# Pooled attention keys in four groups of 32 partitions, pooled copies on ScalarE, and a new instruction order

## The chip, the core and the metric

The kernel runs on one core of one Trainium2 chip. The metric is the device time of one execution in microseconds (us): 299.09 us is the median of three runs before the change (298.9 to 301.79). The engines are named as in the profile: PE (TensorE matmul), PEld (its weight loads), DVE (VectorE), ACT (ScalarE), POOL (GpSimd) and SP (SyncE, which here only issues DMAs).

## What is computed

Inputs are q, k, v of 8 batches, 8 heads, 576 positions and 64 channels, and four matrices of a second stage. Cut to what matters:

```python
q_d, k_d, v_d = mean over groups of 4 positions        # 576 -> 144
out_d   = softmax(q_d @ k_d.T / 8) @ v_d               # pooled attention, 144 x 144 per head
out_up  = repeat(out_d, 4)                             # back to 576 positions
out_loc = softmax(band(q @ k.T / 8)) @ v               # only |i - j| < 4
x = out_up + out_loc                                   # heads side by side: 8 x 576 x 512
theta = x @ w_theta
y = w_tok_r @ (x * cos(theta)) + w_tok_i @ (x * sin(theta))
u = x + y
out = u + relu(u @ w_ch)
```

## The kernel before

All 8 batches run through a software pipeline. Iteration b of the outer loop (b = 0 to 8) works on three batches at once: the attention of batch b, the transposes of q and k of batch b+1 (`turns`), and the second stage's mixing and output of batch b-1. Each stage is a generator that issues a few instructions and yields; a string of letters, one for each step, says which generator goes next. The strings are written out by hand: FIRST for iteration 0, SECOND for 1, PERIOD for 2 to 6, LAST for 7 and END for 8. `pin` (L640) then ties every instruction to the one before it on its engine, so the order of each engine's queue is exactly the order of issue, and every engine takes its queue in that order.

The letters: A (a in iteration 0) is `turns(b+1)`, S `scores`, N `pooled_out`, V `outputs`, T `transposes`, H `phases`, Z `modulate`, X `mix` of batch b-1, R `channels` of b-1, O `store` of b-1, C the casts of loaded inputs of b+2 (POOL), L the loads of b+3 (SP), and W in iteration 0 the loading and transposing of the token matrices.

What the steps of the prediction touch, with lines of the kernel before:

- `turns`, for batches 2 to 7 in 12 steps: four matmuls (L331) transpose 96 positions of q or k and pool them in the same pass into one PSUM bank `pstr`; ACT copies the transposed part (L334), DVE the pooled part (L335) into qdT or kdT. Batches 0 and 1 take eight wider steps (L307, L312). Its last step pools v: five matmuls of 512 columns (L349) in two groups of 90 and 54 pooled positions, each copied by ACT into vd (L355).
- `scores`: pooled scores are 16 matmuls (L368, keys in two groups of 90, the second padded with zeros; queries are 144 columns), taken through Exp by ACT in three instructions (L379 twice, L388). Five band steps follow: eight matmuls (L400), Exp (L408), and two masks on POOL (L421, L423).
- `pooled_out`: two halves of 16 matmuls each, 65 columns wide (L437): 8 heads, 2 key groups. Column 65 gives the softmax's sum. DVE divides (L444, L445).
- `outputs` (psup L462, psloc L467, DVE L474 to L483), `transposes` (xTps L500, DVE L505), `phases` (psth L517, Sin twice on ACT, L524 and L525), `modulate` (DVE L533), `mix` (psu L553, eight steps of ten matmuls, DVE L559), `channels` (psr L573 or L586, psx L578 or L593, Relu on ACT L598), `store` (DVE L608, then DMA).
- PSUM: `w2` gives two tiles of two banks, `w1` four tiles of one bank, each from one pool with that many buffers (L65 to L72).

Of the kernel before, what the change touches and what calls it, by code (L numbers as in the profile page):

```python
# [2 lines left out]

# [5 lines left out]
FP32 = mybir.dt.float32  # L9
BF16 = mybir.dt.bfloat16  # L10
AF = mybir.ActivationFunctionType
ALU = mybir.AluOpType

P = 128
# [21 lines left out]
TP = TR // 4  # L36
TW = TR + TP

KG = [(0, 90), (90, 54)]

OS = [0, 128, 256, 384, 512]
OC = [128, 128, 128, 128, 64]
# [3 lines left out]
def kernel(  # L46
# [15 lines left out]
    work = ctx.enter_context(tc.tile_pool(name="work", bufs=2))  # L62
    xpool = ctx.enter_context(tc.tile_pool(name="xpool", bufs=1))
    moep = ctx.enter_context(tc.tile_pool(name="moep", bufs=2))
    ps2 = ctx.enter_context(tc.tile_pool(name="ps2", bufs=2, space=bass.MemoryType.PSUM))  # L65
    ps1 = ctx.enter_context(tc.tile_pool(name="ps1", bufs=4, space=bass.MemoryType.PSUM))

    def w2(name):
        return ps2.tile([P, 2, 512], FP32, tag="w2", name=name)

    def w1(name, dt=FP32):
        return ps1.tile([P, 512 if dt == FP32 else 1024], dt, tag="w1", name=name)  # L72


    staged = {}
# [39 lines left out]
    for i in range(2):  # L115
        t = const.tile([P, NCH, H, 66], BF16, name=f"v_w{i}")
        nc.vector.memset(t[:, :, :, 64:65], 1.0)
        v_ws.append(t)
    vds = []
    for i in range(2):  # L120

        t = const.tile([90, 2, H, 66], BF16, name=f"vd{i}")
        nc.vector.memset(t[:, 1, :, :], 0.0)
        nc.vector.memset(t[:, 0, :, 64:65], 1.0)
        nc.vector.memset(t[0:54, 1, :, 64:65], 1.0)
        vds.append(t)
    kdTs = []
    for i in range(2):
        t = const.tile([P, 4, 180], BF16, name=f"kdT{i}")
        nc.vector.memset(t[:, :, SD:180], 0.0)  # L130
        kdTs.append(t)

    def cast(b, engines):

# [64 lines left out]


    PU = []
    for lo, hi, sh, w in ((0, 120, 0, 90), (4, 124, 59, 120)):
        r = const.tile([P, w], BF16, name=f"pu{lo}")
        nc.vector.memset(r, 0.25)
        nc.gpsimd.affine_select(out=r, in_=r, compare_op=ALU.is_ge, fill=0.0,
                                base=4 * sh, pattern=[[-4, w]], channel_multiplier=1)
        nc.gpsimd.affine_select(out=r, in_=r, compare_op=ALU.is_ge, fill=0.0,
                                base=3 - 4 * sh, pattern=[[4, w]], channel_multiplier=-1)
        if lo:
            nc.gpsimd.affine_select(out=r, in_=r, compare_op=ALU.is_ge, fill=0.0,  # L210
                                    base=-lo, pattern=[[0, w]], channel_multiplier=1)
        nc.gpsimd.affine_select(out=r, in_=r, compare_op=ALU.is_ge, fill=0.0,
                                base=hi - 1, pattern=[[0, w]], channel_multiplier=-1)
        PU.append(r)

    def pool_mat(g, c):
        o = 0 if c == 0 else 59 - (KS[c] - 360 * g) // 4
        return PU[min(c, 1)][0:KW[c], o:o + KG[g][1]]


    band = []
# [70 lines left out]
    def turns(b):  # L292

        q_tm, k_tm, v_w = inputs[b]
        qT = work.tile([P, 4, S], BF16, tag="qT", name=f"qT{b}")
        kT = work.tile([P, 4, S], BF16, tag="kT", name=f"kT{b}")
        qdT = work.tile([P, 4, SD], BF16, tag="qdT", name=f"qdT{b}")
        kdT = kdTs[b % 2]
        parts[b] = (qT, kT, qdT, kdT)

        pairs = ((q_tm, qT, qdT), (k_tm, kT, kdT))

        def wide_turn(n, hh):
            tm, To, Tdo = pairs[n]
            ps = w2(f"pstr{n}{hh}_{b}")
            for r in range(NTR):
                nc.tensor.matmul(  # L307
                    out=ps[:, r // 3, (r % 3) * TR:(r % 3) * TR + TR],
                    lhsT=tm[:, r, 2 * hh:2 * hh + 2, :], rhs=ip[:, 0:TR], start=True, stop=True,
                )  # L310
            for r in range(NTR):
                nc.tensor.matmul(  # L312
                    out=ps[:, 0, 3 * TR:3 * TR + SD],
                    lhsT=tm[:, r, 2 * hh:2 * hh + 2, :], rhs=pw[:, r, :],
                    start=(r == 0), stop=(r == NTR - 1),
                )
            src = ps[:, :, 0:3 * TR].rearrange("p k (c w) -> p w k c", w=TR)
            dst = To[:, hh, :].rearrange("p (w k c) -> p w k c", k=2, c=3)
            srcd, dstd = ps[:, 0, 3 * TR:3 * TR + SD], Tdo[:, hh, 0:SD]
            if b == 0 and n == 1:  # L320
                nc.vector.tensor_copy(out=dst, in_=src)
                nc.scalar.copy(out=dstd, in_=srcd)
            else:
                nc.scalar.copy(out=dst, in_=src)
                nc.vector.tensor_copy(out=dstd, in_=srcd)

        def turn(n, c):
            tm, To, Tdo = pairs[n]
            ps = w1(f"pstr{n}{c}_{b}")[:, 0:4 * TW].rearrange("p (hh w) -> p hh w", w=TW)
            for hh in range(4):  # L330
                nc.tensor.matmul(  # L331
                    out=ps[:, hh, :], lhsT=tm[:, c, 2 * hh:2 * hh + 2, :], rhs=ip, start=True, stop=True,
                )
            nc.scalar.copy(out=To[:, :, TR * c:TR * c + TR], in_=ps[:, :, 0:TR])  # L334
            nc.vector.tensor_copy(out=Tdo[:, :, TP * c:TP * c + TP], in_=ps[:, :, TR:TW])  # L335

        for i in range(8 if b < WIDE else 12):
            if b < WIDE:
                wide_turn(i % 2, i // 2)
            else:  # L340
                turn(i // 6, i % 6)
            yield

        vd = vds[b % 2]
        for g, cs in ((0, (0, 1, 2)), (1, (3, 4))):
            m = KG[g][1]
            ps = w1(f"psvd{g}_{b}")
            for c in cs:
                nc.tensor.matmul(  # L349
                    out=ps[0:m, :],  # L350
                    lhsT=pool_mat(g, c),
                    rhs=v_w[0:KW[c], c, :, 0:D],
                    start=(c == cs[0]), stop=(c == cs[-1]),
                )
            nc.scalar.copy(out=vd[0:m, g, :, 0:D], in_=ps[0:m, :].rearrange("p (h d) -> p h d", d=D))  # L355
        yield

    pds, pms, xds, xs = {}, {}, {}, {}

    def scores(b):  # L360

        qT, kT, qdT, kdT = parts.pop(b)
        pd = pds[b] = work.tile([90, 2, H, SD], BF16, tag="pd", name=f"pd{b}")
        pms[b] = []

        def pooled_scores(dst, kk, hh):
            for par in range(2):
                nc.tensor.matmul(  # L368
                    out=dst(par),
                    lhsT=kdT[64 * par:64 * par + 64, hh, 90 * kk:90 * kk + 90],  # L370
                    rhs=qdT[64 * par:64 * par + 64, hh, :],
                    start=True, stop=True,
                )

        for kk in range(2):
            ps = w2(f"psSd{kk}_{b}")
            for hh in range(3):
                pooled_scores(lambda par: ps[0:90, par, SD * hh:SD * hh + SD], kk, hh)
            nc.scalar.activation(  # L379
                out=pd[:, kk, 0:6, :].rearrange("p (j e) w -> p e j w", e=2),  # L380
                in_=ps[0:90, :, 0:3 * SD].rearrange("p e (j w) -> p e j w", w=SD),
                func=AF.Exp, scale=SCL,
            )
            yield
        ps = w2(f"psSd2_{b}")
        for kk in range(2):
            pooled_scores(lambda par: ps[0:90, par, SD * kk:SD * kk + SD], kk, 3)
        nc.scalar.activation(  # L388
            out=pd[:, :, 6:8, :].rearrange("p k e w -> p e k w"),
            in_=ps[0:90, :, 0:2 * SD].rearrange("p e (k w) -> p e k w", w=SD),  # L390
            func=AF.Exp, scale=SCL,
        )
        yield
# [34 lines left out]
    def pooled_out(b):  # L428
# [3 lines left out]
        for g in range(2):  # L432
            ps = w2(f"psnd{g}_{b}")
            pv = ps[:, :, 0:260].rearrange("p e (j w) -> p e j w", w=65)
            for h in range(H):
                for kk in range(2):
                    nc.tensor.matmul(  # L437
                        out=pv[0:120, h // 4, h % 4, :],
                        lhsT=pd[:, kk, h, 24 * g:24 * g + 120],
                        rhs=vd[:, kk, h, 0:65],  # L440
                        start=(h % 4 == 0 and kk == 0), stop=(h % 4 == 3 and kk == 1),
                    )
            rd = work.tile([120, 2, 4], FP32, tag="rd", name=f"rd{g}_{b}")
            nc.vector.reciprocal(out=rd, in_=pv[0:120, :, :, 64])  # L444
            nc.vector.tensor_tensor(  # L445
# [157 lines left out]
    def store(b):  # L603
# [14 lines left out]


    FIRST = (  # L620
        "aWallaWaaalaSlllaWlaccSSNcWSWlcNSlcVSVlAlVcSAAcklTTlkkWVSWTAcAHWTVAHWcZHccWTkkZAkCckWkkkZCHWAkWCCWHC"
        "WLLLCAZLLWLWWCCZCLWLLLL"
    )
    SECOND = (
        "ASAXSAXSAXANSXAXAVASXSXSNTROSAACXRCAAOVRHOTVCVHLTVCRLHTZTCLCHZZHCLZRZOLOCCSLLLLL"
    )
    PERIOD = (
        "SSXXAXSAASAANXANASAAXVSAAXSTCVXASCCVHXCCTVROHTCVRLOHTRZHOTCCLLRLZOZZHCRZSOLLLLLL"
    )
    LAST = (  # L630
        "SSXXXSSXNSXSVXSVTXSVRHONTXTVHVSHTRTZOZROHZHZZRORO"
    )
    END = (
        "XXXXXXXROROXRORROO"
    )

    last = {}
# [68 lines left out]
```

## Time and profile before

| what | value |
|---|---|
| median of 3 runs | 299.09 us |
| the profiled execution | 298.93 us |
| its span, first to last instruction | 297.2 us |
| mean granted TensorE clock | 0.976 of full speed |
| busy: PE, DVE, ACT, POOL | 275.5, 204.1, 189.7, 159.5 us |

The page also cuts the span into 40 slices of 7.43 us; a digit is the busy share in tenths, and PEclk is the granted clock in tenths:

```profile
DVE  4433868657895598658883888468855986488642
ACT  1145458775668776776788667877787678565312
POOL 5666774478841399327960798059904900580000
PEclk9998579999999999999999999999999999999999
DMA  7999999999999953897189906992220012000304
```

The clock fell to about half between 30 and 37 us and was full afterwards. The DMA engines are full for the first 16 slices, while inputs of the first batches are fetched ahead. Durations of matmuls in the profile run from start to a modelled end and overlap; what a matmul costs PE is the distance from its start to the start of the next.

### The profile page before, as it was taken

To read this page: it belongs to the slowest core of one execution; us is meant where nothing else is said; L and a number is where in the kernel's file an instruction comes from. 1 tells how busy PE (TensorE), PEld (TensorE's weight loads), DVE (VectorE), ACT (ScalarE), POOL (GpSimd) and SP (SyncE) were. 2 spreads that over 40 slices of the span, in tenths; PEclk is the share of its full clock that TensorE was granted. 3 is DMA by queue.
4 is the path that set the end of the run, shared out by engine and by line. 5 is a ranking of instruction groups with operands and counts; after the bars stand their busy time and mean duration, and the time that the engine had idled before them with its cause. 6 is when DMAs were issued, how large, how long until landed. Compare 5 with 4: busy or idle time off the path is not lost.

```text
span 297.2 us, 7393 instructions
## 1 busy us (share of the span) xinstructions
PE 275.5 (93%) x2946; PEld 197.4 (66%) x2946; DVE 204.1 (69%) x466; ACT 189.7 (64%) x304; POOL 159.5 (54%) x186
## 2 busy tenths in 40 slices
PE   2497899999989999999999999999999999999993
PEld 1385587687656876587657876687668766776762
DVE  4433868657895598658883888468855986488642
ACT  1145458775668776776788667877787678565312
POOL 5666774478841399327960798059904900580000
PEclk9998579999999999999999999999999999999999
DMA  7999999999999953897189906992220012000304
GB/s 188 228 298 276 254 198 189 256 195 200 186 253 188 235 109 102 180 224 144 36 199 218 199 5 181 216 208 46 79 82 3 3 67 94 2 35 3 124 23 138
DMA packets 107826, 43.57 MB, mean 147 GB/s; under 512 B 97424, under 2 KB 101520, under 8 KB 107792
## 3 DMA queue, kind: packets, MB, share of 16 engines
q1 hardware_dynamic: 107792, 43.10, 69.4%
q8 instruction: 23, 0.38, 0.6%
q14 instruction: 11, 0.09, 0.1%
HBM read 33.65 MB, written 9.44 MB: 145 GB/s over the span
## 4 chain that ended last, share of the span: by engine, by line
PE 75%; DMA 7%; POOL 4%; SPq 4%; DVE 4%; ACT 2%; issue 1%; DVEq 0%; POOLq 0%; ACTq 0%
PE psu L553 26%; PE psth L517 11%; PE psr L573 8%; PE pstr L331 6%; PE psnd L437 4%; PE psS L400 3%; DMA q<-in_q_dram 3%; PE psvd L349 3%; SPq L107 3%; PE psloc L467 3%; PE psup L462 3%; PE xTps L500 2%; DMA w<-in_moe_w_theta_dram 2%; PE psx L578 2%; PE psSd L368 2%
## 5 line engine op out<-in xcount | busy, mean ns | idle before, releaser
L553 PE MATMUL psu<-WT,z 120*128 120x288 bf16 (+1 forms) x640 | 87.0, 286 | 0.2 <-ACT rel L598 0.2
L421 POOL TENSOR_SCALAR_AFFINE_SELECT pm<-pm 128x1024 bf16<-128x1024 bf16 (+1 forms) x32 | 33.7, 1053 | 73.7 <-ACT pm L408 73.6
L553 PEld LDWEIGHTS <-z 120*128 120x128 bf16 (+1 forms) x640 | 59.9, 98 | 15.9 <-issue 0.2
L408 ACT ACTIVATE pm<-psS 128x1024 bf16<-128x1024 f32 (+1 forms) x40 | 39.4, 984 | 18.0 <-PE psS L400 16.7
L559 DVE TENSOR_TENSOR uT<-psu,xT 128x288 bf16<-128x288 f32 x64 | 29.0, 454 | 26.2 <-PE psu L553 25.9
L517 PE MATMUL psth<-wth,xT 128*120 128x512 bf16 (+1 forms) x160 | 41.3, 381 | 0.2 <-DVE xT L505 0.2
L524 ACT ACTIVATE cs<-psth,pihc 120x512 bf16<-120x512 f32 (+1 forms) x40 | 27.4, 686 | 16.0 <-PE psth L517 13.8
L598 ACT ACTIVATE rel<-psr 128x512 f32<-128x512 f32 (+1 forms) x40 | 22.0, 554 | 23.1 <-PE psr L573 19.7
L423 POOL TENSOR_SCALAR_AFFINE_SELECT pm<-pm 128x1024 bf16<-128x1024 bf16 (+1 forms) x32 | 34.1, 1064 | 2.2
L573 PE MATMUL psr<-wch,uT 128*128 128x512 bf16 x128 | 33.0, 378 | 0.0
L608 DVE TENSOR_TENSOR osb<-rel,psx 128x512 f32<-128x512 f32 (+1 forms) x40 | 24.9, 630 | 7.6 <-ACT rel L598 7.6
L533 DVE TENSOR_TENSOR z<-cs,x 120x1024 bf16<-120x1024 bf16 (+1 forms) x40 | 29.2, 756 | 0.8 <-ACT cs L525 0.8
L476 DVE TENSOR_TENSOR tmp<-psloc,rl 120x512 bf16<-120x512 f32 (+1 forms) x40 | 27.6, 691 | 1.4
L483 DVE TENSOR_TENSOR x<-tmp,psup 120x512 bf16<-120x512 bf16 (+1 forms) x40 | 27.4, 686 | 1.4
L525 ACT ACTIVATE cs<-psth 120x512 bf16<-120x512 f32 (+1 forms) x40 | 23.5, 588 | 0.0
L517 PEld LDWEIGHTS <-xT 128*120 128x120 bf16 (+1 forms) x160 | 18.0, 131 | 7.9 <-DVE xT L505 0.7
L153 POOL CAST v_w<-v 128x1024 bf16<-128x1024 f32 x16 | 18.4, 1166 | 7.7 <-DMA v<-in_v_dram 5.2
L149 POOL CAST k_tm<-k 96x1024 bf16<-96x1024 f32 x18 | 18.3, 1040 | 7.7 <-DMA k<-in_k_dram 7.7
L334 ACT CAST kT<-pstr 128x384 bf16<-128x384 f32 x36 | 16.0, 483 | 9.8 <-PE pstr L331 9.8
L467 PEld LDWEIGHTS <-pm 128*128 128x128 bf16 (+1 forms) x320 | 16.6, 105 | 7.0 <-DVE tmp L476 1.9
L335 DVE CAST qdT<-pstr 128x96 bf16<-128x96 f32 x36 | 9.2, 256 | 16.1 <-ACT qT L334 14.8
L334 ACT CAST qT<-pstr 128x384 bf16<-128x384 f32 x36 | 16.2, 484 | 4.9 <-PE pstr L331 4.9
(89 smaller groups left out, 474.4 us busy)
## 6 DMA issues: line engine op xcount, KB each, us to landing
v<-in_v_dram SPq DMA_DIRECT2D x32, 256.0 KB, 5.8
out_dram<-osb SPq DMA_DIRECT2D x32, 256.0 KB, 2.2
q<-in_q_dram SPq DMA_DIRECT2D x36, 192.0 KB, 4.8
k<-in_k_dram SPq DMA_DIRECT2D x36, 192.0 KB, 5.1
q<-in_q_dram SPq DMA_DIRECT2D x8, 288.0 KB, 4.8
k<-in_k_dram SPq DMA_DIRECT2D x8, 288.0 KB, 6.9
v<-in_v_dram SPq DMA_DIRECT2D x8, 200.0 KB
wt<-in_moe_w_tok_r_dram SPq DMA_DIRECT2D x4, 288.0 KB, 6.9
```

The source lines that it names most:

```text
L334: nc.scalar.copy(out=To[:, :, TR * c:TR * c + TR], in_=ps[:, :, 0:TR])
L408: nc.scalar.activation(out=pv, in_=ps[0:kw].rearrange("p e (j w) -> p (e j) w", w=P)[:, :, 0:qn], func=AF.Exp, scale=SCL,)
L421: nc.gpsimd.affine_select(out=pv, in_=pv, compare_op=ALU.is_ge, fill=0.0, base=off, pattern=[[0, 8], [-1, qn]], channel_multiplier=1)
L423: nc.gpsimd.affine_select(out=pv, in_=pv, compare_op=ALU.is_ge, fill=0.0, base=6 - off, pattern=[[0, 8], [1, qn]], channel_multiplier=-1)
L476: nc.vector.tensor_tensor(out=tmp[0:cnt].rearrange("p (j e d) -> p e j d", e=2, j=4), in0=pv[0:cnt, :, :, 0:D], in1=rl[0:cnt].unsqueeze(3) ...
L483: nc.vector.tensor_tensor(out=x[0:cnt], in0=tmp[0:cnt], in1=up[0:cnt], op=ALU.add)
L517: nc.tensor.matmul(out=th[0:cnt, :], lhsT=xT[:, dc, QS[c]:QS[c] + cnt], rhs=wth[:, dc, :], start=(dc == 0), stop=(dc == 3),)
L524: nc.scalar.activation(out=cs[0:cnt, 0, :], in_=th[0:cnt], func=AF.Sin, bias=pihc[0:cnt], scale=1.0)
L533: nc.vector.tensor_tensor(out=z[0:cnt, c, :, :], in0=css.pop((b, c))[0:cnt], in1=xs[b][c][0:cnt].unsqueeze(1).to_broadcast([cnt, 2, DM]), ...
L553: nc.tensor.matmul(out=ps[:, 0:288], lhsT=z[0:QC[c], c, ri, P * dc:P * dc + P], rhs=WT[0:QC[c], ri, c, cols], start=(c == 0 and ri == 0), ...
L559: nc.vector.tensor_tensor(out=uT[:, dc, cols], in0=ps[:, 0:288], in1=xT[:, dc, cols], op=ALU.add)
L573: nc.tensor.matmul(out=psr, lhsT=uT[:, dc, P * c:P * c + P], rhs=wch[:, dc, :], start=(dc == 0), stop=(dc == 3),)
```

## The change

Pooled keys are laid out in four groups of 32 partitions. Groups 0 to 3 hold 30 pooled keys each (120 of 144), and the last 24 form a fifth group, whose scores for heads 0 to 3 and 4 to 7 are stacked in four blocks of 32 partitions. The matching values are a block diagonal (`vd[:, 1]`): POOL multiplies the pooled values of the last chunk by `own`, which is 1 on a head's own 32 partitions and 0 elsewhere.

- Pooling v: four matmuls with 32 output partitions and 512 columns (L354), each into its own 32 partitions, and four with 128 columns (L357). ACT copies twice (L359 512 wide, L361 128 wide), POOL multiplies twice (L363).
- Pooled scores: eight matmuls with 128 keys (L382) and eight with 32 keys (L402). Exp is two instructions (L392, L408) in place of three.
- Pooled output: each half has eight matmuls of 65 columns (L456) and two of 260 (L462).
- Pooled copies of `turns` go from DVE to ACT (L338); kdT is now one plain buffer, from which DVE makes the padded kdP in two copies (L347, L348).
- PSUM: two tags of one buffer for `w2` and four for `w1`, taken in a fixed cycle.
- All five order strings are new. In iteration 0 the load of w_ch now comes ahead of v of batch 1 and q of batch 2; before, it came after both. In PERIOD each engine's queue is new too; two places are used below. At the end of a period PE's queue is the last psth, psr, psx, psr, psx, psr (L610), psx, psva (L354), psvb (L357), one pstr, psSd (L382), one pstr, then psu. DVE's is z twice, osb, z twice, osb three times, the two kdP copies, then uT.

```diff
-KG = [(0, 90), (90, 54)]
+KP = 32
...
+    turn2, turn1 = itertools.cycle("ab"), itertools.cycle("abcd")
     def w2(name):
-        return ps2.tile([P, 2, 512], FP32, tag="w2", name=name)
+        return ps2.tile([P, 2, 512], FP32, tag="w2" + next(turn2), name=name)
...
-            nc.vector.tensor_copy(out=Tdo[:, :, TP * c:TP * c + TP], in_=ps[:, :, TR:TW])
+            nc.scalar.copy(out=Tdo[:, :, TP * c:TP * c + TP], in_=ps[:, :, TR:TW])
...
+        nc.vector.tensor_copy(out=kdP[:, :, 0:4, 0:30], in_=kdT[:, :, 0:120].rearrange("p h (g m) -> p h g m", g=4))
+        nc.vector.tensor_copy(out=kdP[:, :, 4, 0:24], in_=kdT[:, :, 120:144])
+        yield
         vd = vds[b % 2]
-        for g, cs in ((0, (0, 1, 2)), (1, (3, 4))):
...
+        psa, psb = w1(f"psva_{b}"), w1(f"psvb_{b}")
+        for c in range(4):
+            nc.tensor.matmul(out=psa[KP * c:KP * c + KP, :], lhsT=PU[min(c, 1)], rhs=v_w[:, c, :, 0:D],
+                             start=True, stop=True)
+        for c in range(4):
+            nc.tensor.matmul(out=psb[KP * c:KP * c + KP, 0:2 * D], lhsT=PU[1][0:KW[4], :],
+                             rhs=v_w[0:KW[4], 4, c::4, 0:D], start=True, stop=True)
+        nc.scalar.copy(out=vd[:, 0, :, 0:D], in_=psa.rearrange("p (h d) -> p h d", d=D))
+        nc.scalar.copy(out=last4, in_=psb[:, 0:2 * D].rearrange("p (s d) -> p s d", d=D))
+        for s in range(2):
+            nc.gpsimd.tensor_tensor(
+                out=vd[:, 1, 4 * s:4 * s + 4, 0:D],
+                in0=last4[:, s, :].unsqueeze(1).to_broadcast([P, 4, D]),
+                in1=own.unsqueeze(2).to_broadcast([P, 4, D]),
+                op=ALU.mult,
+            )
...
-                    lhsT=kdT[64 * par:64 * par + 64, hh, 90 * kk:90 * kk + 90],
+                    lhsT=kdP[64 * par:64 * par + 64, hh, 0:4, :],
...
+        for h in range(H):
+            par, r = h % 2, KP * (h % 4)
+            nc.tensor.matmul(
+                out=ps[r:r + KP, h // 4, SD:2 * SD],
+                lhsT=kdP[64 * par:64 * par + 64, h // 2, 4, :],
+                rhs=qdT[64 * par:64 * par + 64, h // 2, :],
+                start=True, stop=True,
+            )
...
             for h in range(H):
-                for kk in range(2):
...
+                nc.tensor.matmul(
+                    out=pv[0:120, h // 4, h % 4, :],
+                    lhsT=pd[:, h, 24 * g:24 * g + 120], rhs=vd[:, 0, h, 0:65],
+                    start=(h % 4 == 0), stop=False,
+                )
+            for e in range(2):
+                nc.tensor.matmul(
+                    out=pv[0:120, e, :, :],
+                    lhsT=pd[:, H + e, 24 * g:24 * g + 120], rhs=vd[:, 1, 4 * e:4 * e + 4, 0:65],
+                    start=False, stop=True,
+                )
...
     PERIOD = (
-        "SSXXAXSAASAANXANASAAXVSAAXSTCVXASCCVHXCCTVROHTCVRLOHTRZHOTCCLLRLZOZZHCRZSOLLLLLL"
+        "ASAXXSSAXSAANAXVSXAVSCAXASTTVAHNXVHTXASTZHVRCHCOTRZZAOLHCSCLCCLCLLLZZRROCOROLLLL"
     )
     END = (
-        "XXXXXXXROROXRORROO"
+        "XXXXXXXXRORORORORO"
     )
```

## The prediction

> **What bounds the kernel now.** First the page's busy table, then the same by stretches of the span (the bounds taken from the chain of waits, where a new period begins with the matmuls of L349), then PE's own waits.
>
> ```profile
> PE 275.5 (93%) x2946; PEld 197.4 (66%) x2946; DVE 204.1 (69%) x466; ACT 189.7 (64%) x304; POOL 159.5 (54%) x186
> ```
> ```profile
> 80.00:90.00 10.00, 8.72 (x78) 4.91 (x78) 9.74 (x20) 6.98 (x12) 4.35 (x5) 1.00 1.16 237
> ...
> 154.33:185.67 31.34, 31.34 (x351) 22.39 (x352) 23.32 (x55) 23.71 (x40) 19.82 (x19) 1.00 0.77 155
> ```
> ```profile
> PE pstr L307 <- DVE q_tm L143: 4.8, 1, 4.8
> PE pstr L307 <- DVE qdT L325: 3.5, 2, 2.9
> ```
>
> In the stretches the columns are length, then busy time of PE, PEld, DVE, ACT, POOL, granted clock, DMA share, GB/s. In a period (iterations 2 to 6) PE is busy 31.34 of 31.34 us at full clock, ACT 23.71, DVE 23.32. PE's large waits are all in the first 14 us; from about 50 to 290 us only 80 to 95 us shows gaps, about 2 us in all, while DVE is at 9.74 of 10. So a microsecond taken from PE's queue in a period shortens the run, unless another engine then comes late.
>
> What PE's steps cost is read from start to start in PE's timeline of one period (start, duration, engine, line):
>
> ```profile
> 153.59 0.63 PE L586 MATMUL psr<-wch,uT 128*64 128x256 bf16 x8
> 154.05 0.28 PE L593 MATMUL psx<-ident,uT 128*64 128x128 bf16 x4
> 154.26 1.39 PE L349 MATMUL psvd<-v_w,pu 128*90 128x512 bf16 x5
> 155.58 0.57 PE L368 MATMUL psSd<-qdT,kdT 64*90 64x144 bf16 x12
> 156.09 2.63 PE L553 MATMUL psu<-WT,z 120*128 120x288 bf16 x20
> ...
> 160.08 0.32 PE L368 MATMUL psSd<-qdT,kdT 64*90 64x144 bf16 x4
> 160.34 0.59 PE L331 MATMUL pstr<-ip,q_tm 96*128 96x120 bf16 x8
> ...
> 161.63 1.02 PE L437 MATMUL psnd<-vd,pd 90*120 90x65 bf16 x16
> 162.48 1.39 PE L553 MATMUL psu<-WT,z 120*128 120x288 bf16 x10
> 163.71 0.37 PE L331 MATMUL pstr<-ip,q_tm 96*128 96x120 bf16 x4
> 163.92 1.02 PE L437 MATMUL psnd<-vd,pd 90*120 90x65 bf16 x16
> 164.78 0.38 PE L331 MATMUL pstr<-ip,k_tm 96*128 96x120 bf16 x4
> ```
>
> Pooling v costs 155.58 - 154.26 = 1.32 us, pooled scores 0.51 + 0.26 = 0.77, pooled output 0.85 + 0.86 = 1.71: 3.80 us of each period. Two prices come out too. Twenty matmuls of 288 columns before L331 take 158.55 - 156.09 = 2.46 us, 0.123 each or 0.427 ns a column. And L586, eight matmuls of 256 columns into alternating halves of the output partitions, takes 0.46 us where 8 x 256 x 0.427 is 0.87: matmuls into different output partitions do run side by side here.
>
> **The change on PE, per batch.** *Pooling v*: four matmuls of 512 columns, one after another, would be 0.87 us and four of 128 columns 0.22, 1.09 together; at L586's ratio (0.46/0.87) 0.58; side by side four ways 0.27. I take 0.45, nearer to the four-way end because four groups are addressed where L586 has two. It saves 0.87 (0.23 to 1.05). *Pooled scores*: L368 costs 0.51/12 = 0.0425 us a matmul; sixteen at that price are 0.68. The eight narrow ones could be as quick as 0.24 in all (four pairs of 61 ns, 144 columns each) or as slow as 0.49 (one after another). It saves 0.09 (-0.06 to 0.19). *Pooled output*: a 65-column matmul costs 0.855/16 = 0.053; eight of them and two of 260 columns (0.111 each) are 0.65 a half, 1.30 for both. It saves 0.41; the bound is 0.3 to 0.45. Together 1.37 us a batch, between 0.5 and 1.7.
>
> One rule speaks against the narrow scores. The Trainium skill, "TensorEngine Tiling (Array Packing)", section "Restrictions and Gotchas", says that matmuls on different row halves must write different PSUM banks and cannot use one bank at once. In the code L368 sends its two row halves to two banks, while the new L402 sends both to the same bank. If that makes the eight run singly, by the column price above they cost 0.49 and not 0.34, 1.0 us over seven batches, and the sum would be 293.8 in place of 292.8; no trace here shows two row halves in one bank.
>
> Batches 1 to 7 do this work where PE is the bound (L349 of batch 1 starts at 54.9 us), so 7 x 1.37 = 9.6 us (3.3 to 11.8). Batch 0 does it around 20 to 30 us; there the chain of waits goes through DMA and POOL, and I count nothing.
>
> **Other engines.** ACT gains 12 copies of 96 elements a period and DVE loses them:
>
> ```profile
> L334 ACT CAST qT<-pstr 128x384 bf16<-128x384 f32 x36 | 16.2, 484 | 4.9 <-PE pstr L331 4.9
> ...
> L335 DVE CAST qdT<-pstr 128x96 bf16<-128x96 f32 x36 | 9.2, 256 | 16.1 <-ACT qT L334 14.8
> ```
>
> ACT's 576-wide copy (L324) takes 640 ns and the 384-wide one 484, 0.81 ns an element, so 96 elements are about 250 ns; two copies in a row took 0.85 us, not 0.97, so up to 0.1 overlaps. That is 1.9 to 3.0 us. One Exp of 884 ns goes, and the second v copy shrinks from 579 to about 270: 1.2 us off. ACT stands at 24.4 to 25.5 of some 30 us, not the bound. DVE loses 12 x 0.256 = 3.1 us and gains two kdP copies; nearest are 0.40 us (480 elements from PSUM, L505) and 0.15 (96 elements, L186), so 0.2 to 0.55, taken as 0.4. POOL gains two products of 256 elements, between 0.26 (L205, 90 elements) and 0.62 us (L233, 512) each; POOL idles 9.31 us at the start of a period before its first mask, and psnd, which needs them, comes after four psu: hidden. If POOL were late, its masks would be as well. Exchanging the buffers' tags takes nothing: the same eight banks are used in turn.
>
> **The new wait.** At a period's end DVE is now in PE's way. psSd (L382) needs kdP, and kdP stands on DVE behind the last osb. Laying the new queues out with the durations above, from the end of the last psth (t=0): ACT's two Sin take until 1.3; DVE's last z until 2.0; three osb (0.6, 0.6, 0.35) until 3.65; kdP until 4.05. PE: psr, psx, psr, psx, the last psr and psx are 0.86+0.22+0.86+0.22+0.46+0.21 = 2.83, then psva and psvb 0.45 and pstr 0.24: 3.52. PE waits about 0.5 us, and everything in its queue behind (pstr, psu) with it. If z or osb runs ahead by 0.6 it is nothing; if they run behind, or the handovers take 0.1 each, 0.9. Over the six starts of iterations 2 to 7: 3.0 us back (0 to 5.4). If pooling v does not run side by side, PE arrives later by that time and this wait vanishes: the two uncertainties partly cancel.
>
> **The first two iterations.** w_ch, 1.05 MB, now goes ahead of v of batch 1 and q of batch 2. The 2.4 MB of v and q were issued from 36.0 and cast on landing by 54.0, 133 GB/s; w_ch and two pieces of k, 1.44 MB, were there at 59.1, 282 GB/s. So it delays them 3.7 to 7.9 us. Against it: five pieces of q and k of batch 1 now stand ahead of the seventh token-matrix piece, at which the SP queue stood from 21.9 to 25.7 (3.8 us), and q of batch 2 was cast by 55.05 and first wanted at 57.19 (2.1). I take 0.5 us lost, near where delay and cover meet, between 2 gained and 5.8 lost (7.9 less 2.1). Iteration 1 has its eight psu early and then a tail where DVE (psnd, x, xT, osb, z: some 17 us against 15 of PE) paces: its gaps of 2 us stay, no more and no less, within 1 us. END's first psr now follows all eight psu; nothing waits there that did not.
>
> **Sum**, against the profiled execution of 298.93 (1.73 beyond its span; 0.16 below the median): 298.93 - 9.6 + 3.0 + 0.5 = 292.8.
>
> **Rivals.** (1) *No new wait* (0.25): DVE, relieved of its copies, is ahead and kdP is in time: 298.93 - 9.6 + 0.5 = 289.8. For it: DVE has slack in a period; against: the last three osb depend on the last psr. (2) *Narrow matmuls do not run side by side* (0.17): pooling v and scores save 0.2 together, pooled output 0.42: 7 x 0.6 = 4.2, no wait for kdP, 0.5 for the loads: 295.2. Against: L586. (3) *ACT becomes the pace, slower* (0.06): ACT idles 31.34 - 23.71 = 7.6 us a period. If its order forces all of that, a period is 24.4 to 25.5 + 7.6 = 32 to 33.1, 0.7 to 1.8 over the old, and six such periods with 0.5 for the loads give 303 to 310; say 305. It decides once forced idle exceeds 6.9 us. Against: PE ends most of ACT's idle time, and PE's pace itself shortens. (4) The change does not lower PE's work at all, because weight loads or switching between shapes eat it: 298 to 300 (0.05), for it that the columns streamed stay 6,944 a batch, against it L586 and the nine matmuls fewer a batch.
>
> **How the numbers follow.** Forecast 0.47, with 290.5 to 295; the others as given. About 1% (3 us) is what a measurement can tell from no change: faster needs less than 296.1. All of the forecast but a tail, rival 1, and two thirds of rival 2 lie there: 0.82. Same: the rest of rival 2, rival 4, tails: 0.12. Slower 0.06. The range of 288 to 297.5 takes in forecast and rivals 1 and 2, with the bounds of the loads.
>
> **What would show it.** psva to the next pstr at 0.3 to 0.6 us; psnd at 0.65 a half; PE waiting for DVE kdP six times at about 0.5; a period of 30.0 to 30.7; ACT near 25 in it. A period over 31 with ACT above 27 proves me wrong by rival 3; a PE gap of several us near 55 to 60 is the loads.

## The result and the profile after

| | before | after |
|---|---|---|
| median, us (4 runs each) | 299.19 | 309.58 |
| lowest to highest, us | 298.9 to 301.79 | 307.51 to 312.5 |
| ratio to before, 95% interval | | 1.030 [1.023, 1.038] |
| profiled execution, us | 298.93 | 309.22 |
| a middle period, us | 31.34 | 34.20 |

The kernel became 3% slower, where 292.8 us had been forecast. The ratio goes by means and leaves out the execution of 312.5 us, which was in a slower state that some executions show, so it isn't the quotient of the medians. The first view is the page: busy time by engine, and the granted clock in 40 slices, now of 7.69 us.

```profile
PE 273.9 (89%) x2865; PEld 195.7 (64%) x2874; DVE 207.1 (67%) x423; ACT 192.6 (63%) x368; POOL 168.2 (55%) x203
...
PEclk9999999599999999799998999799989999999999
```

PE does a little less than before in a longer span, and the clock now falls five times: deeply in the eighth slice (54 to 61 us), and then once about every 34 us, that is once a period. The stretch of one period, from the start of pooling v (L354) to its next start (columns as in the prediction's table of stretches), and PE's waits (total, times, longest) say the same:

```profile
124.72:158.92 34.20, 32.03 (x343) 22.64 (x341) 24.11 (x45) 24.67 (x50) 20.96 (x23) 0.95 0.72 142
```
```profile
PE psx L617 <- DVE osb L632: 8.4, 4, 2.1
...
PE psSd L382 <- DVE kdP L347: 0.5, 1, 0.5
```

PE has gaps of 34.20 - 32.03 = 2.17 us in a period that had none, and the large wait is not the one that was forecast: psx, not psSd, waits, four times 2.1 us. The timeline around it (start, duration, engine, line; in brackets the idle time just before and what ended it) shows where the time goes, first PE, then DVE and POOL:

```profile
121.75 0.63 PE L610 MATMUL psr<-wch,uT 128*64 128x256 bf16 x8
124.49 0.30 PE L617 MATMUL psx<-ident,uT 128*64 128x128 bf16 x4 [2.11 <-DVE osb L632]
124.72 0.40 PE L354 MATMUL psva<-v_w,pu 128*32 128x512 bf16 x4
125.09 0.24 PE L357 MATMUL psvb<-v_w,pu 100*32 100x128 bf16 x4
125.26 0.38 PE L334 MATMUL pstr<-ip,q_tm 96*128 96x120 bf16 x4
125.62 0.36 PE L382 MATMUL psSd<-qdT,kdP 64*128 64x144 bf16 x6
125.91 0.58 PE L334 MATMUL pstr<-ip,q_tm 96*128 96x120 bf16 x4
126.28 4.08 PE L577 MATMUL psu<-WT,z 120*128 120x288 bf16 x20
130.29 0.24 PE L382 MATMUL psSd<-qdT,kdP 64*128 64x144 bf16 x2
130.46 0.31 PE L402 MATMUL psSd<-qdT,kdP 64*32 64x144 bf16 x8
130.70 0.40 PE L420 MATMUL psS<-qT,kT 64*128 64x128 bf16 x8
...
117.67 1.27 DVE L557 TENSOR_TENSOR z<-cs,x 120x1024 bf16<-120x1024 bf16 x2
...
119.49 4.35 DVE L557 TENSOR_TENSOR z<-cs,x 120x1024 bf16<-120x1024 bf16 x2
123.76 1.60 DVE L632 TENSOR_TENSOR osb<-rel,psx 128x512 f32<-128x512 f32 x3
...
118.85 3.01 POOL L161 CAST k_tm<-k 96x1024 bf16<-96x1024 f32 x3 [6.21 <-PE pstr L334]
121.80 2.94 POOL L165 CAST v_w<-v 128x1024 bf16<-128x1024 f32 x2
```

The new arithmetic is as quick as forecast: pooling v, from 124.72 to 125.26, costs 0.54 us. Ahead of it PE stands for 2.11 us. The narrow psx (L617), the transposed last piece of u, needs a PSUM bank that the first of the three osb (DVE's sums of rel and psx for the output) empties, and these stand on DVE behind two z that take 4.35 us; the two z before them took 1.27. During those 4.35 us POOL casts k and v of the batch two ahead without a pause. POOL had idled 6.21 us until a matmul of L334 released it: it may overwrite k_tm only when PE has transposed the last piece of k out of it. The page's group of z shows the loss as a mean, 1084 ns where it had been 756:

```profile
L557 DVE TENSOR_TENSOR z<-cs,x 120x1024 bf16<-120x1024 bf16 (+1 forms) x40 | 42.3, 1084 | 1.4 <-ACT cs L549 1.3
```

The gap costs a second time. The twenty psu behind it go from 126.28 to 130.29, 4.01 us where they had taken 2.46 (granted clock 0.50 from 126 to 129): 1.6 us more. 34.20 - 2.1 - 1.6 = 30.5 is the period that was forecast.

### The profile page after: what moved, and what is told of

Same layout as the page of the kernel before. It is cut to its first block, busy times and chain, and to the rows that moved or that the text cites. A ratio compares the mean times of both kernels' runs of the same rounds, so it can differ in the third digit from the quotient of the medians.

```text
span 307.5 us, 7263 instructions
## 1 busy us (share of the span) xinstructions
PE 273.9 (89%) x2865; PEld 195.7 (64%) x2874; DVE 207.1 (67%) x423; ACT 192.6 (63%) x368; POOL 168.2 (55%) x203
## 5 line engine op out<-in xcount | busy, mean ns | idle before, releaser
L577 PE MATMUL psu<-WT,z 120*128 120x288 bf16 (+1 forms) x640 | 94.0, 302 | 0.1
L577 PEld LDWEIGHTS <-z 120*128 120x128 bf16 (+1 forms) x640 | 63.9, 103 | 19.5 <-issue 0.3
L557 DVE TENSOR_TENSOR z<-cs,x 120x1024 bf16<-120x1024 bf16 (+1 forms) x40 | 42.3, 1084 | 1.4 <-ACT cs L549 1.3
L622 ACT ACTIVATE rel<-psr 128x512 f32<-128x512 f32 (+1 forms) x40 | 22.2, 554 | 17.7 <-PE psr L597 16.4
L165 POOL CAST v_w<-v 128x1024 bf16<-128x1024 f32 x16 | 20.2, 1276 | 9.8 <-DMA v<-in_v_dram 8.6
L337 ACT CAST kT<-pstr 128x384 bf16<-128x384 f32 x36 | 17.2, 478 | 7.0 <-PE pstr L334 6.9
L337 ACT CAST qT<-pstr 128x384 bf16<-128x384 f32 x36 | 17.8, 495 | 5.5 <-PE pstr L334 5.5
L363 POOL TENSOR_TENSOR vd<-last,own 128x256 bf16<-128x256 bf16 x16 | 9.8, 635 | 20.6 <-ACT last L361 20.6
```

Source lines behind the costliest of these rows:

```text
L557: nc.vector.tensor_tensor(out=z[0:cnt, c, :, :], in0=css.pop((b, c))[0:cnt], in1=xs[b][c][0:cnt].unsqueeze(1).to_broadcast([cnt, 2, DM]), ...
L577: nc.tensor.matmul(out=ps[:, 0:288], lhsT=z[0:QC[c], c, ri, P * dc:P * dc + P], rhs=WT[0:QC[c], ri, c, cols], start=(c == 0 and ri == 0), ...
```

## The experiments

The theory after the first look: the new PERIOD puts the last step on k so late that POOL's casts fall beside DVE's z, z waits for POOL, PE waits for osb, and the clock falls after that wait. The rivals: it is the wait for kdP, it is the clock alone, it is the fixed turn of the PSUM banks, or it is the loads of the first iterations. Ratios are to the kernel before, run on the same chip.

| kernel | median, us | ratio [95%] | middle period, us |
|---|---|---|---|
| a1_old_period | 308.62 | 1.024 [1.014, 1.033] | 32.74 |
| a2_k_buffers | 296.83 | 0.989 [0.981, 0.996] | 30.57 |
| a3_fill | 306.21 | 1.018 [1.011, 1.026] | 32.59 |
| a4_before_new_period | 347.36 | 1.158 [1.149, 1.167] | 41.0 |
| b1_early_turn | 303.01 | 1.008 [1.003, 1.012] | 32.2 |
| b2_before_late_turn | 318.19 | 1.049 [1.038, 1.060] | 36.0 to 37.3 |
| v1_w_ch_later | 295.82 | 0.984 [0.978, 0.989] | 30.57 |
| u1_pooled_copies_dve | 301.96 | 1.005 [1.001, 1.009] | 31.3 |
| u2_psum_pools | 294.57 | 0.981 [0.976, 0.986] | 30.40 |
| v2_vd_on_dve | 296.41 | 0.981 [0.974, 0.988] | 30.56 |
| c1_after_pools | 311.48 | 1.036 [1.032, 1.040] | 34.16 |
| c2_pools_w_ch_k_buffers | 294.73 | 0.979 [0.975, 0.984] | 30.4, one of 32.2 |

**Two buffers for k** (the kernel after, one word changed):

```diff
-        k_tm = work.tile([TR, NTR, H, D], BF16, tag="k_tm", bufs=1, name=f"k_tm{b}")
+        k_tm = work.tile([TR, NTR, H, D], BF16, tag="k_tm", bufs=2, name=f"k_tm{b}")
```

> The kernel after with two buffers for k_tm, so that POOL's casts of k need not wait for the last k turn on PE (24.7 us of waiting in the trace). Theory: the casts of k and v run some 6 us earlier, beside the first z and not the last; z3 and z4 fall to 0.7 us, the wait at psx goes or falls under 1 us, 294 to 302. Rival (z is slow for another reason than POOL): z3 stays at 2.9 us, 308 to 311.

It took 296.83 us, 12.8 less than the kernel after in these medians. Order and arithmetic are those of the kernel after; only what POOL must wait for is different. Its timeline at the same place, POOL, DVE and PE:

```profile
113.67 3.46 POOL L161 CAST k_tm<-k 96x1024 bf16<-96x1024 f32 x3
...
121.18 0.68 DVE L557 TENSOR_TENSOR z<-cs,x 120x1024 bf16<-120x1024 bf16 x1
...
123.36 0.30 PE L617 MATMUL psx<-ident,uT 128*64 128x128 bf16 x4
123.59 0.40 PE L354 MATMUL psva<-v_w,pu 128*32 128x512 bf16 x4
...
125.19 2.62 PE L577 MATMUL psu<-WT,z 120*128 120x288 bf16 x20
```

The casts of k now start at 113.67, 9.92 us ahead of psva; in the kernel after they start 5.87 ahead. The z beside no cast takes 0.68, psx waits for nothing, and the twenty psu take 2.56 at full clock. The period is 30.57 us, in the forecast's 30.0 to 30.7. POOL still collides with z (882 ns on average), but with earlier z, and PE hardly waits for what stands behind those. The release of k_tm is therefore the cause of the loss in the periods.

**The gap filled** (the kernel after, 36 matmuls into an unused half of the same PSUM bank between L610 and psx for batches 1 to 5, which is at the end of iterations 2 to 6, so that PE works where it had waited; at the end of iteration 6 it had not waited):

```diff
+                for i in range(36 if 1 <= b <= 5 else 0):
+                    hf = i % 2
+                    nc.tensor.matmul(
+                        out=psr[64 * hf:64 * hf + 64, w:2 * w], lhsT=uT[:, 0, 512:576],
+                        rhs=wch[:, 0, 0:w], start=True, stop=True,
+                    )
```

> 36 extra matmuls (256 columns, alternating halves, into the unused half of the psr bank, read by nobody) stand between L610 and the last psx in iterations 1 to 5, some 2 us of PE work where PE sat idle 2.1 us. Theory (the idle gap makes the granted clock fall to half for some 3.3 us, which costs 1.6 us at each of four period starts): the clock stays at 1.0 at the period starts, the 20 psu that took 4.08 us take 2.5, the time is 302 to 304. Rival (the clock falls for some other reason, such as the load of the matmuls itself): the 20 psu stay at 4.0, the time is 309 or more.

The total missed its 302 to 304: 306.21. The period answered: 32.59 us (127.71 to 160.30) against 34.20, 1.61 less, at a granted clock of 1.00 throughout. So of the 3.63 us that two buffers gained per period (34.20 - 30.57), 1.61 were the clock and 2.0 the wait itself. Less came of it in all, for three reasons. Iteration 1, which has no filling, took 40.53 us and not 39.18: its psvb waited 2.39 us for POOL's cast of v, where the profile of the kernel after shows a wait of 0.31. Iteration 2 took 34.49 and not 32.94: at its start the clock fell behind waits of 1.26 and 0.36 us. And in iteration 6 the 36 matmuls filled no gap and cost 1.96 us.

**The old order in the new kernel**, and **the new order in the old one** (each takes the PERIOD of the other):

```diff
-        "ASAXXSSAXSAANAXVSXAVSCAXASTTVAHNXVHTXASTZHVRCHCOTRZZAOLHCSCLCCLCLLLZZRROCOROLLLL"
+        "SSXXAXSAASAANXANASAAXVSAAXSTCVXASCCVHXCCTVROHTCVRLOHTRZHOTCCLLRLZOZZHCRZSOLLLLLL"
```

> The kernel after with only the PERIOD string of the kernel before. Theory: the casts end before most of z, no wait at psx; but psSd now stands right behind psva, and kdP on DVE behind three z and the last osb, so PE waits 1.5 to 2 us for kdP at each period start, with or without a fall of the clock: 295 to 303. Rival (the new work itself is slow, whatever the order): 308 to 311 with the same wait at psx.

> The kernel before with only the PERIOD string of the kernel after. Theory (the order is at fault: the last k turn stands late, so POOL's casts of k and v run beside DVE's z, z takes up to 2.9 us, osb and then PE's psx come late): z is slow here too, PE waits about 2 us at psx at the period's end, 304 to 310 us. Rival (the new matmuls, the copies on ACT or the padded keys are at fault, the order is innocent): 298 to 301.

With the old order the collision is gone (z is back at 723 ns on average) and psx waits no longer, but the time was 308.62, a miss. Other waits took the place of the first, as PE's waits show:

```profile
PE psSd L382 <- DVE kdP L347: 5.9, 6, 1.2
...
PE psr L597 <- ACT cs L549: 3.5, 5, 0.7
```

The first is the wait that the prediction had named, here 1.0 us a period: the old order has psSd directly behind psvb, with no pstr between them. The old order was written for a kernel without kdP, and doesn't suit the new one. The clock falls at two of the six starts of periods: in iteration 2 behind waits of 1.56 and 0.67 us, and in iteration 6 behind 0.30 and 1.01 us, while the same two waits in the three iterations between left it at 1.00.

The reverse exchange gives no evidence on the order in its total of 347.36 us: the old `scores` has one step more, so each later S of the string means another instruction, and psloc alone waits 23.7 us for masks. Two details can be used. psx waits for osb there too, four times 2.2 us, with z at 936 ns. And what the clock does is not a matter of a wait's length alone, as PE's waits within one period show:

```profile
165.23 0.55 PE L467 MATMUL psloc<-v_w,pm 100*96 100x65 bf16 x8 [2.87 <-POOL pm L423]
175.03 0.30 PE L593 MATMUL psx<-ident,uT 128*64 128x128 bf16 x4 [2.23 <-DVE osb L608]
...
190.12 0.42 PE L467 MATMUL psloc<-v_w,pm 128*128 128x65 bf16 x8 [1.74 <-POOL pm L423]
```

The granted clock is 1.00 from 160 to 190 us, behind the waits of 2.87 and 2.23 us, and 0.50 from 191 to 193, behind the one of 1.74. It is the same in the other three periods with these waits.

**One letter of each PERIOD.** The last A of the string is the step of `turns` that transposes the last piece of k. In the new kernel it goes directly behind the A before it; in the old kernel it goes to a late place, nothing else.

```diff
-        "...VHTXASTZHVRCHCOTRZZAOLHC..."
+        "...VHTXAASTZHVRCHCOTRZZOLHC..."
```
```diff
-        "...AAXSTCVXASCCVHX...LLRLZOZZHCRZSO..."
+        "...AAXSTCVXSCCVHX...LLRLZOZZAHCRZSO..."
```

> The kernel after with one letter of PERIOD moved: the last k turn goes right behind the one before it, some 5 us earlier in PE's queue; k_tm keeps one buffer. Theory (where this turn stands decides when POOL may cast k, and so beside which z): as with two buffers, the wait at psx goes, the clock stays full at the period starts, a period is 30.5 to 31 us, the time 295 to 300. Rival (a second buffer helped through the loads that it lets go earlier, not through the casts): 306 to 311.

> The kernel before with one letter of PERIOD moved: the last k turn goes 24 letters later, to where the kernel after has it; nothing else. Theory: the casts of k and v land on the last z here too, z and osb run late, PE waits at the end or start of each period and the clock falls behind a wait of 2 us: 306 to 320. Rival (only the new work or the rest of the new order is at fault): 298 to 301.

The early step gave 303.01 us, between the two forecasts: psx waits no longer and the clock doesn't fall at the start of a period, but the casts now lie beside z of the first blocks, x comes late behind them, and xTps waits for DVE's x 8.3 us in seven places. The collision moved, and a part of the loss stayed.

The late step made the old kernel, with its old arithmetic, 5% slower: 318.19 us. Its timeline shows the whole chain in a kernel that has no kdP, no narrow matmuls and no turn of the banks (POOL, DVE, PE):

```profile
154.10 3.01 POOL L149 CAST k_tm<-k 96x1024 bf16<-96x1024 f32 x3 [5.79 <-PE pstr L331]
...
154.95 4.14 DVE L533 TENSOR_TENSOR z<-cs,x 120x1024 bf16<-120x1024 bf16 x2
159.02 0.24 DVE L335 CAST kdT<-pstr 128x96 bf16<-128x96 f32 x1
...
159.32 0.59 PE L349 MATMUL psvd<-v_w,pu 128*54 128x512 bf16 x2 [2.30 <-DVE kdT L335]
...
160.54 4.05 PE L553 MATMUL psu<-WT,z 120*128 120x288 bf16 x20
```

A late last k step releases the casts, two z take 4.14 us, PE waits 2.30 and then runs its twenty psu at half clock (3.89 us to the next start). At 0.6 us each the two z would have been through before PE needed kdT. One letter of the order is enough for it.

**The prices by themselves.** A small program of its own: eight z alone, beside six casts of POOL, beside six masks; eight osb beside six casts; then PE in blocks of 64 matmuls with pauses of known length between them.

> A probe that leaves the whole computation out. First part: eight DVE products shaped like z (bf16, both inputs in SBUF) alone, beside six POOL casts shaped like k's, beside six POOL masks; then eight sums shaped like osb (fp32, one input in PSUM) beside six casts. Theory (z and POOL's casts cannot run at once): alone z takes 0.6 to 0.7 us; beside the casts the two take turns, some z of 1.5 to 3 us, and both together last about the sum of both, 10 us and more; osb beside casts stays at 0.6 to 0.7. Rival (both slow down each other evenly): every z near 1.2 us, osb too. Second part: PE works 13 us, pauses for one to five ACT copies, and works again, twice over. Theory: pauses of 0.8 and 1.4 us leave the clock full, pauses over 2 us halve it for some 3 us; in between it depends on when the pause falls. Rival: no pause under 3 us has any effect.

The timeline of DVE and POOL, then of PE, where 13.97 us is a block at full clock:

```profile
10.13 4.90 DVE L71 TENSOR_TENSOR z<-cs,x 120x1024 bf16<-120x1024 bf16 x8
...
15.51 9.83 DVE L71 TENSOR_TENSOR z<-cs,x 120x1024 bf16<-120x1024 bf16 x8
...
25.83 10.22 DVE L71 TENSOR_TENSOR z<-cs,x 120x1024 bf16<-120x1024 bf16 x8
...
36.54 4.86 DVE L77 TENSOR_TENSOR osb<-rel,psx 128x512 f32<-128x512 f32 x8
...
15.35 8.24 POOL L82 CAST k<-k 96x1024 bf16<-96x1024 f32 x6
...
36.37 5.93 POOL L82 CAST k<-k 96x1024 bf16<-96x1024 f32 x6
...
37.86 13.97 PE L107 MATMUL wk<-ch,lh 128*128 128x512 bf16 x63 [1.32 <-ACT ch L115]
53.80 13.97 PE L107 MATMUL wk<-ch,lh 128*128 128x512 bf16 x62 [1.97 <-ACT ch L115]
70.40 15.66 PE L107 MATMUL wk<-ch,lh 128*128 128x512 bf16 x63 [2.62 <-ACT ch L115]
...
135.28 15.66 PE L107 MATMUL wk<-ch,lh 128*128 128x512 bf16 x63 [1.97 <-ACT ch L115]
153.56 13.97 PE L107 MATMUL wk<-ch,lh 128*128 128x512 bf16 x63 [2.62 <-ACT ch L115]
```

A z costs 0.61 us alone (4.90/8). Beside casts the eight take 9.83, but the casts end at 23.59, and two of the z run after them; the six beside them took (9.83 - 2 x 0.61)/6 = 1.43 each. Six casts take 8.24 us beside z and 5.93 beside osb, which itself isn't touched (0.61). z and casts together last from 15.35 to 25.34, 9.99 us, little less than the two one after the other, 4.90 + 5.93 = 10.83: they nearly take turns, as the theory had it, and both sides lose. A pause of 1.97 us cost nothing the first time and 15.66 - 13.97 = 1.69 us the second; 2.62 cost 1.69 the first time and nothing the second. These 1.69 us are about the 1.6 that the periods of the kernel after pay.

**Loads of the first iterations.** On top of the two buffers for k, w_ch's load goes behind q of batch 2:

```diff
-        nc.sync.dma_start(out=w32[1], in_=moe_w_ch.rearrange("(c p) e -> p c e", p=P))
...
+                if ri == 1 and c == 0:
+                    nc.sync.dma_start(out=w32[1], in_=moe_w_ch.rearrange("(c p) e -> p c e", p=P))
```

> Two buffers for k_tm as in the run a2, and w_ch is loaded behind q of batch 2, as in the kernel before. Theory (w_ch ahead of v of batch 1 and q of batch 2 makes their casts and PE's first steps of iteration 1 late, and the gap halves the clock for some 6 us): no clock fall near 56 us, 3 to 5 us less than a2, 291 to 294. Rival (DMA has room, the fall near 56 us has another cause): 296 to 298.

It gave 295.82, above its 291 to 294, and 1.0 below the two buffers alone, with intervals that overlap. PE's gaps near 54 to 56 us are gone, but psnd then waits 2.6 us for POOL's products for vd, which stand behind casts of v that wait for their own load, and the clock falls in this wait instead (0.72 from 70 to 72 us, 0.50 from 72 to 76). Taking those products to DVE for batch 1 was the next trial:

```diff
-            nc.gpsimd.tensor_tensor(
+            (nc.vector if b == 1 else nc.gpsimd).tensor_tensor(
                 out=vd[:, 1, 4 * s:4 * s + 4, 0:D],
```

> v1 (two buffers for k_tm, w_ch behind q of batch 2), and for batch 1 alone DVE in place of POOL makes the two products for vd, since in v1 psnd waited 2.6 us for them behind POOL's casts of v, which wait for DMA, and the clock fell after it. Theory: no clock fall in the first 95 us, 2 to 4 us less than v1, 291.5 to 294. Rival (the tail of iteration 1 waits for DVE anyway and takes the gain back): 295 to 296.

296.41: no gain; psloc then waits 4.1 us for POOL's masks, and the clock falls once more, later again (0.62 from 76 to 78 us).

**The other parts of the change.** On top of the two buffers, the pooled copies go back to DVE:

```diff
-            nc.scalar.copy(out=Tdo[:, :, TP * c:TP * c + TP], in_=ps[:, :, TR:TW])
+            nc.vector.tensor_copy(out=Tdo[:, :, TP * c:TP * c + TP], in_=ps[:, :, TR:TW])
```

> Two buffers for k_tm as in a2, but the pooled copies of turns stay on DVE as in the kernel before. Theory: the copies are no part of the loss, ACT has room and DVE has not; DVE's 3.1 us more in each period come in the first half, where it waits for psu: 296 to 299. Rival (the copies on ACT hold up the chain): under 295.

301.96, some 5 us more than with the copies on ACT, and above both forecasts. DVE comes late with x and xd, and PE waits for both:

```profile
PE xTps L524 <- DVE x L507: 3.8, 4, 1.6
PE psup L486 <- DVE xd L469: 3.0, 6, 0.9
```

So this part of the change is worth some 5 us in the new order, which was written for it. The PSUM pools go back to two and four buffers without a fixed turn, on top of the two buffers for k (u2), in the kernel after (c1), and with w_ch's later load (c2):

```diff
-        return ps2.tile([P, 2, 512], FP32, tag="w2" + next(turn2), name=name)
+        return ps2.tile([P, 2, 512], FP32, tag="w2", name=name)
...
-        return ps1.tile([P, 512 if dt == FP32 else 1024], dt, tag="w1" + next(turn1), name=name)
+        return ps1.tile([P, 512 if dt == FP32 else 1024], dt, tag="w1", name=name)
```

> Two buffers for k_tm as in a2, and PSUM tiles from one pool with several buffers each, as in the kernel before; the instructions and their order are those of a2, only the bank of a tile can differ. Theory (the fixed turn is no part of the loss): 295.5 to 298, like a2. Rival (the fixed turn makes tiles wait for a bank while another is free): under 295.

> The kernel after with PSUM tiles from one pool with several buffers each, as in the kernel before; k_tm keeps one buffer, the order is that of the kernel after. Theory (the casts beside z are the main loss, the fixed turn of banks adds a little): z3 still 2.9 us, PE still waits near the period's end, somewhat shorter; 302 to 308. Rival (the fixed turn is the main loss, since it ties the last psx to a bank that a late osb holds while others are free): the wait goes, 294 to 299.

> All three together: two buffers for k_tm, w_ch behind q of batch 2, PSUM from pools. Theory (what is left of the loss after a2 and u2 is the load order of iteration 0): 291 to 293.5. Rival (in u2 the loads were already hidden, as its clock had no fall near 56 us): 294 to 295.5, no better than u2.

The first gave 294.57 us, in the rival's range, and the shortest period, 30.40; its profiled execution, at 292.19 the quickest of its four, has full clock in every slice, the others 0.985 to 0.993. In the kernel after it changed nothing (311.48; psx waits 8.9 us in four, period 34.16), so the turn is no part of the loss. The third, 294.73, adds nothing to the first. Whether the turn costs the kernel with two buffers some 2 us is not settled, since the intervals of the two overlap. The versions with the pools and two buffers for k beat both kernels: 0.981 [0.976, 0.986] of before, some 15 us below the kernel after.

## Why the prediction was wrong

The profiled execution took 309.22 us, 16.4 more than the forecast. Counted from psva to psva against the old stretches less the forecast's terms, iteration 1 took 39.18 us and not 36.13 - 1.37 + 0.5 = 35.26 (3.9 more; it had started 2.2 earlier, a gain that was neither forecast nor followed up), iteration 2 1.8 more, iterations 3 to 5 3.7 more each, iteration 6 1.5 more, the rest 0.2. That pattern is the mechanism's: iteration 2 ends with the first wait of 2.1 and has no slow psu yet, three periods have both, and iteration 6 has the slow psu but no wait at its end, there being no casts left.

**The arithmetic was right.** Pooling v costs 0.54 us (forecast 0.45), pooled scores 0.29 + 0.17 + 0.24 = 0.70 (0.68), half a pooled output 134.00 - 133.33 = 0.67 (0.65):

```profile
133.33 0.58 PE L456 MATMUL psnd<-vd,pd 128*120 128x65 bf16 x8
...
134.00 0.38 PE L334 MATMUL pstr<-ip,q_tm 96*128 96x120 bf16 x4
```

Together 3.80 - 0.54 - 0.70 - 1.34 = 1.22 us a batch are saved, where 1.37 were forecast. Rivals 2 and 4 fall by these numbers. That a period without its losses comes to the forecast's 30.5 (31.34 - 1.37 + 0.5) is partly luck: its 0.5 us of waiting for kdP aren't there, 0.15 less is saved, and what takes the rest was not followed up.

**The rule that was weighed did not decide.** The narrow eight of L402, both row halves in one bank, take 130.70 - 130.46 = 0.24 us, the quick end of the prediction's bounds. The Trainium skill, "TensorEngine Tiling (Array Packing)", section "Restrictions and Gotchas", names it as a thing that can't happen at once; as a cost in time it doesn't show in this trace, and the measurement stands.

**ACT was right.** It is busy 24.67 us in a period (24.4 to 25.5 forecast); PE's large waits are not for it. Rival 3 falls.

**"The new wait" is the step that failed.** It laid out the end of the period on PE, ACT and DVE from the old durations, with "DVE's last z until 2.0", and left POOL out; what the trace shows in its place is two z of 4.35 us beside POOL's casts, 2.1 us of waiting at psx, and 1.6 us of half clock behind it. (Its own sum is also 0.1 long: 2.0 + 0.6 + 0.6 + 0.35 is 3.55 and not 3.65, 0.6 us over six starts.) The mechanism it named, psSd behind kdP, exists: 1.0 us a period under the old order (a1), 2.5 us in six under u2, little in the kernel after. What it did not ask is who is released by PE's last transpose of k. The code has k_tm with one buffer, POOL's casts of the next k wait for that transpose, and the new order moved it from well before the z into the middle of them. The old z group, taken by shape, gave a hint, 774 ns on average and 0.68 for most single ones: some z were already slow beside POOL. The second half of the cost, the clock, had stood in the old profile as well: by stretches it is 0.50 from 28 to 40 us, longer than the page's slices suggest. The prediction gave no price to a gap beyond its own length. In the old kernel that early fall costs nothing that shows: executions with a mean clock of 0.965 to 0.977 took 298.5 to 302.3 us, those with 0.996 to 1.00 took 299.4 to 302.9.

**The first iterations were mis-sized.** The term was 0.5 us lost, with a bound of 5.8; iteration 1 took 3.9 more than forecast. Here too the waits are small and the clock makes them large:

```profile
54.30 0.98 PE L334 MATMUL pstr<-ip,q_tm 96*128 96x120 bf16 x8 [0.74 <-POOL q_tm L161]
56.05 0.98 PE L334 MATMUL pstr<-ip,q_tm 96*128 96x120 bf16 x8 [0.78 <-ACT qdT L338]
56.83 4.66 PE L577 MATMUL psu<-WT,z 120*128 120x288 bf16 x20
```

PE waits 0.74 and 0.78 us, for POOL's casts of q of batch 2 and what hangs on them (the third starts at 57.03 us, before at 54.01). The clock is half from within the first of these on (1.00 from 52 to 54 us, 0.58 from 54 to 55), and the next twenty psu cost 4.49 us (to 61.32), 2.0 over their price: 3.5 of the 3.9. The prediction's clue, "a PE gap of several us near 55 to 60 is the loads", pointed to the right place and to too simple a sign. Moving the load cleared these gaps and gained almost nothing, because the next late cast took their place; which of the small waits of iterations 0 and 1 costs what stays open.

## What to carry to other kernels

When an order of instructions is changed, list for every moved matmul who waits for the buffer that it was the last to read: in this kernel one step moved past three z released five casts of POOL into a stretch where DVE had no gap, and a second buffer took away the whole loss of the periods. Lay out all engines around the place, POOL too, and price two engines that work on SBUF at once by a row where they did so. And a PE gap of about 2 us is to be priced at up to 2 + 1.6 us, for the clock that may fall behind it, depending on the moment, and not at its length.

## What the runs showed of the hardware

**z on DVE and casts or masks on POOL nearly take turns.** z, with both inputs in SBUF, went from 0.61 to 1.43 us beside POOL's casts, and eight of them took 10.22 us in place of 4.90 beside six masks, which had not been expected; the casts went from 0.99 us beside osb (5.93/6) to 1.37 beside z (8.24/6). osb, with one input in PSUM, stayed at 0.61. In the kernel after two z beside the casts took 4.35. The Trainium skill, "SBUF — State Buffer", section "Who interferes with whom", states that a DVE instruction with two SBUF inputs contends with a POOL instruction that reads SBUF; the probe agrees.

**The clock falls after shorter gaps than had been thought, and not by their length alone.** In the kernel after, gaps of 2.1 us before the same psx were followed by half clock in four of four periods; in a4, gaps of 2.23 us before the same psx were in none of four, and gaps of 1.74 us further on in four of four. Periods of one kernel are alike, so four of them are less than four separate trials. In the probe pauses of 1.97, 2.62 and 3.27 us each did it once in two trials, and 0.67 to 1.38 us never in four. Shorter gaps preceded a fall too: 0.30 and 1.01 us at the start of a period in one of four (a1), and 0.31 and 0.74 us in iteration 1 of the kernel after; that these caused it was not tried. The Trainium skill, "TensorE: Matmul & The Clock Gate", section "What's actually happening", gives half rate after at least one idle window of about 3.4 us, in windows that run free of the kernel. The dependence on the moment agrees with the probe and with a4; the length does not, since 1.74 us was enough here, and the measurement decides.
